# Attention stage of a fused attention, MLP and expert kernel: where ScalarE's exponential and VectorE's side work stand in the scheduler's order

## The chip, the cores and the metric

The kernel runs on one core of a Trainium2 chip. The metric is the time of one execution in microseconds of device time. Three executions of the kernel before took 960.75, 962.94 and 966.66 us; their median is 962.94 us.

## The reference

Causal attention over 4 batches, 8 heads, 576 positions and a head size of 64 is mixed with a memory read-out and goes through a dense MLP and then through one of eight expert MLPs. The change lies in the attention.

```python
scores = scale * np.matmul(q, k.transpose(0, 1, 3, 2))
scores = np.where(causal, -1000000000.0, scores)
a = np.exp(scores - scores.max(-1, keepdims=True))
a /= a.sum(-1, keepdims=True) + 1e-09
local = np.matmul(a, v)
q_p = phi(q)                       # phi(x) = where(x > 0, x, exp(x) - 1) + 1
mem_out = einsum(q_p, M_prev) / (einsum(q_p, z_prev)[..., None] + 1e-06)
attn = g * mem_out + (1 - g) * local          # g = sigmoid(beta), per head
x = attn.transpose(0, 2, 1, 3).reshape(B * S, H * D)
x = np.maximum(x @ w_in, 0.0) ** 2 @ w_out
...
```

After this each row of x is routed to its best of 8 experts (normalized dot products, softmax weight), and the expert's two matmuls with a ReLU between them give the output.

## The kernel before, in words

**Stages.** The attention comes first (about 0 to 384 us of the trace); the first half of the dense MLP is laid between its steps. The rest of the MLP, the routing and the experts follow. Each float32 matmul is made of three matmuls of rounded parts (names ending in `h` and `l` are the high and the low part of a tile).

**Pairs and units.** The heads are taken in 16 pairs of two, numbered 0 to 15 here. A pair has nine units, in the order of ORDER: unit 0 has the last 64 rows of both heads (`h` is None, tile `A8`), then come (head, block of 128 rows): (0,3), (1,3), (0,0), (1,0), (0,2), (1,2), (0,1), (1,1). A unit is a chain over four engines:
- TensorE makes the scores into `ps` (`scores`, L446, matmuls L476);
- VectorE copies them to `A` under the mask and takes the row minimum of their negatives into `nm` in the same instruction (L480, "the minimum" below; a second short instruction reads `nm` out);
- ScalarE makes the exponential of `A` in place with its row sums `sm` (L486);
- VectorE makes the reciprocal of the sums (L494 and L495, or L489 and L490), for both heads of a block at once;
- GpSimd scales `A` by it (L437);
- five units later TensorE transposes `A` into a PSUM tile `pt` (`turn`, L442). It is one of two buffers of the pool `psT` (tag T, L195), which also hold the transposes of the features of the next pair (`tk`, `tq`, `t2`, `tp`, `t3`);
- ScalarE copies `pt` to SBUF (`ATa`, `ATb`, `AT`, L619), and eight units after its scores the unit is multiplied with the values (`values`, L538, L570).

**The features of the next pair** (`prep`, L301) run beside the units: `e` is the exponential of q (ScalarE, L349); `phi` (L352 to L354) finishes it on VectorE; GpSimd multiplies by z into `u` (L358); `norm` (L387) sums `u` on VectorE into `nr` (L388), adds and inverts it (L390, L392); GpSimd multiplies `e` by `nr` (L396); TensorE transposes `e` into `tp` (L403). The transposes `t2` of the last rows are copied by ScalarE to `hk` and `qbh` (L368, L371), and VectorE makes their low parts `kl` and `qbl` (L374, L377).

**The MLP's part.** `step` lays one half step of the MLP into most units: the first layer (12 matmuls L742; then ScalarE's ReLU `r` L746, VectorE's square L750, ScalarE's rounding `gh` L751 and VectorE's remainder `gl` L752), or the second layer (6 matmuls L776 to L778, which read `gh` and `gl`). In pairs 9, 11, 13 and 15 the next chunk of x is split: `xh` on ScalarE (L719), `xl` on VectorE (L720).

**What sets the order.** The loop over t (t = 9 * pair + unit, from L607) writes instructions unit by unit. `later` puts functions aside for a later t and an engine's list: "act0" and "dve0" are run ahead of the unit's minimum and exponential, "act", "dve" and "pool" behind them (`due`, L594). What is written is not always what each engine gets: TensorE's order is always the written one; ScalarE's, VectorE's, GpSimd's and SyncE's are the written ones only up to t = 8 (STRICT = 9, L608), VectorE's and GpSimd's up to t = 71 (FREE = 72, L611). From there on a scheduler places each instruction as early as its own estimates say that its inputs are there. t = 72 is the first unit of pair 8. `pinned` (L79) is a context in which each new instruction of an engine is placed behind the last one written so far for that engine.

In the loop (L628 to L643) the unit whose scores were written last is `here`, the one ahead of it is `before`. The first `next(here)` writes the minimum, the second the exponential; `next(before)` writes the sums' reciprocals and the scaling.

Of the kernel before, what the change touches and what calls it, by code (L numbers as in the profile page):

```python
# [19 lines left out]
ENG = mybir.EngineType  # L20
# [38 lines left out]
FREE = 72  # L59
STRICT, BUSY = 9, {-5: 14, 0: 12, 2: 6, 4: 4, 5: 4, 6: 4, 7: 4}  # L60
# [31 lines left out]
@contextmanager  # L92
def pinned(tc, *engines):

    with ExitStack() as ctx:
        for e in engines:
            last = next((i for i in reversed(tc.nc.cur_bb.bb.instructions) if i.engine == e), None)
            if last is not None:
                ctx.enter_context(tc.issue_after(last))
        yield  # L100
# [87 lines left out]
def attention(tc, sh, q, k, v, M, z, beta, w_in, w_out, mlp, step):  # L188

    nc = tc.nc  # L190
    with ExitStack() as ctx:
# [44 lines left out]
        def load(p):  # L236
            b, hp = divmod(p, NPP)
            qn_, kn_ = naturals.get(p, (qn, kn))
            fetch(p, (k, kn_), (q, qn_))
            zb = st.tile([128, 128], F32, name="zb", tag="zb")  # L240
            nc.sync.dma_start(zb, z[b:b + 1, 2 * hp:2 * hp + 2].rearrange("o h d -> o (h d)").to_broadcast([128, 128]))
            nat[p] = (vns[p % 3], zb, Mts[p % 3], qn_, kn_)

        def load_values(p):
            b, hp = divmod(p, NPP)
            fetch(p, (v, vns[p % 3]))
            for h in range(2):
                hs = slice(h * 64, h * 64 + 64)
                nc.sync.dma_start(Mts[p % 3][hs, hs], M[b, 2 * hp + h])
# [23 lines left out]
        def mix():  # L273

            nc.scalar.activation(g_all, g_all, AF.Exp, scale=-1.0)
            nc.vector.tensor_scalar_add(gi, g_all, 1.0)
            nc.vector.reciprocal(g_all, gi)
            nc.vector.tensor_scalar(g1, g_all, -1.0, 1.0, ALU.mult, ALU.add)
            for h in range(2):
                hs = slice(h * 64, h * 64 + 64)  # L280
                nc.vector.tensor_copy(g2[hs], g1.rearrange("p (a h) -> p h a", h=2)[hs, h])
# [309 lines left out]
        conv = conversions2(nc, st, sh, 0, nc.gpsimd, w_in, w_out)  # L591
        units = [(p, h, r) for p in range(NPAIR) for h, r in ORDER]

        def due(eng):  # L594
            for f in queue.pop((t, eng), ()):
                f()

        def busy(n):

            w = psX.tile([128, 512], F32, name="w", tag="X")  # L600
            for _ in range(n):
                nc.tensor.transpose(w[:, :128], ident, ident)

        here, before, gens, t = None, None, [prep(0)], -EARLY
        while t < len(units) + LP + 5 or queue:
            now[0] = t
            p, i = divmod(t, 9)  # L607
            if t == STRICT:  # L608
                strict.close()
                strict.enter_context(tc.manual_schedule(engines={ENG.DVE, ENG.Pool}))  # L610
            if t == FREE:  # L611
                strict.close()
            if t in BUSY:
                busy(BUSY[t])
            start = START[min(p, 2)]
            if 0 <= p < NPAIR - 1 and i == start:
                gens.append(prep(p + 1))
            for d, x in evacs:
                nc.scalar.copy(d, x)  # L619
            evacs.clear()  # L620
            due("act0")
            if here is not None:
                next(here)
            due("dve0")
            if here is not None:
                next(here)
            if before is not None:
                next(before)  # L628
            before, here = here, None
            if t == MIX:  # L630
                mix()
            if t == AHEAD:
                next(conv)
            due("act")
            due("dve")
            due("pool")
            if t > CONV[0] and t % 9 != CONV[1] and next(conv, conv) is not conv:
                sh.converted += 1
            n = t - LP
            if n % 9 == 0 and (n - 1) // 9 in JOINED:  # L640
                values(*units[n - 1])
            if 0 <= n < len(units) and (n % 9 < 8 or n // 9 not in JOINED):
                values(*units[n])  # L643
            if 0 <= p < NPAIR - 2 and i == 8:
                load_values(p + 2)
            if t % 9 != REST:
                step(t)
            for g in list(gens):
                if next(g, gens) is gens:
                    gens.remove(g)  # L650
            if 0 <= p < NPAIR - 2 and i == start + 5:
                load(p + 2)
            if 0 <= t - LT < len(units):
                turn(*units[t - LT])
            if 0 <= t < len(units):
                here = scores(*units[t])
                next(here)
            for f in behind_scores:
                f()
            behind_scores.clear()  # L660
            t += 1
# [752 lines left out]
def tile_kernel(ctx, tc, q, k, v, M, z, beta, w_in, w_out, emb, tau, w1, w2, out):  # L1414
# [16 lines left out]
    with ExitStack() as mctx:  # L1431
# [17 lines left out]
        with tc.manual_schedule(engines={ENG.PE}):  # L1449
            attention(tc, sh, q, k, v, M, z, beta, w_in, w_out, mlp, step)  # L1450
# [63 lines left out]
```

## Time and profile before

| what | value |
|---|---|
| median of three executions | 962.94 us (960.75 to 966.66) |
| profiled execution: its own time, its span | 954.52 us, 952.4 us |
| TensorE busy | 898.4 us, 94% of the span |
| TensorE's weight loads | 787.3 us, 83% |
| VectorE, ScalarE, GpSimd busy | 594.3 us, 525.0 us, 293.2 us |
| mean granted TensorE clock | 0.989 of full speed |

The span reaches from the first to the last instruction; 2.1 us of the profiled execution lie around it. The profiled execution is 8.4 us below the median of the three others. Starts in the trace are counted from the span's start. A wait is given with the engine and tile that ended it; where an instruction waits for several things, the one that came last is named.

### The profile page before, as it was taken

The numbers are of one execution on the slowest core, as the hardware profiler recorded it, in microseconds if no ns is written. First come the engines' busy times: TensorE is split into PE (matmuls) and PEld (weight loads), VectorE is DVE, ScalarE is ACT, GpSimd is POOL, SyncE is SP. The second block draws the span as 40 slices with busy tenths as digits, with TensorE's granted clock in tenths as the row PEclk, the third lists the DMA queues.
The fourth block names the chain that finished last, engine by engine and source line by source line (L and its number), as shares of the span: only waits on it lengthen the run. The fifth ranks groups of instructions, "written<-read, shape, count | busy, mean of one in ns | idle before, by whom it ended". The sixth has DMA issues, their size and how long they took to land.

```text
span 952.4 us, 19266 instructions
## 1 busy us (share of the span) xinstructions
PE 898.4 (94%) x6319; PEld 787.3 (83%) x6319; DVE 594.3 (62%) x1737; ACT 525.0 (55%) x1363; POOL 293.2 (31%) x356
## 2 busy tenths in 40 slices
PE   7878899999999999999999999999999999999993
PEld 6766677888888888898798888888899999999983
DVE  4689878655555654587527778889772535353551
ACT  4787778776666667576655555665421424242440
POOL 4466657333334432000311111433311311111111
PEclk9999899999999999999999999999999999999997
DMA  6677666444344420244310112521060635352521
GB/s 175 152 176 186 154 158 155 118 101 114 86 110 92 116 56 23 70 153 156 112 62 35 61 45 82 174 67 47 33 222 20 199 113 161 102 174 91 181 78 35
DMA packets 107081, 105.81 MB, mean 111 GB/s; under 512 B 66095, under 2 KB 76335, under 8 KB 106944
## 3 DMA queue, kind: packets, MB, share of 16 engines
q1 hardware_dynamic: 100528, 89.13, 34.0%
q0 software_dynamic: 4544, 13.67, 4.4%
q10 hardware_dynamic: 1872, 1.34, 0.5%
q8 instruction: 66, 1.08, 0.5%
q14 instruction: 71, 0.58, 0.2%
HBM read 70.80 MB, written 14.70 MB: 90 GB/s over the span
## 4 chain that ended last, share of the span: by engine, by line
PE 66%; DVE 14%; issue 7%; DMA 6%; ACT 4%; POOL 2%; SPq 1%; POOLq 0%; ACTq 0%; DVEq 0%
PE ps L742 16%; PE psh L1309 11%; PE y L776 5%; PE y L778 5%; PE y L777 5%; PE ps L476 4%; PE psy L1325 3%; PE psy L1327 3%; PE psy L1326 3%; PE xo L570 3%; PE pt L442 2%; DMA raw<-in_moe_w_out_dram 2%; DVE A L480 2%; DMA raw<-in_moe_w_in_dram 2%; DVE x L879 1%
## 5 line engine op out<-in xcount | busy, mean ns | idle before, releaser
L437 POOL TENSOR_SCALAR A<-A,sm,g 128x512 f32<-128x512 f32 (+4 forms) x108 | 80.5, 754 | 134.7 <-DVE sm L495 61.0
L486 ACT ACTIVATE A<-A,nm 128x576 f32<-128x576 f32 (+2 forms) x144 | 84.7, 588 | 63.2 <-DVE nm L480 27.2
L742 PE MATMUL ps<-xh,Wh 128*128 128x256 f32 x416 | 118.3, 284 | 0.4 <-ACT r L746 0.4
L742 PE MATMUL ps<-xh,Wl 128*128 128x256 f32 x416 | 117.5, 282 | 0.0
L742 PE MATMUL ps<-xl,Wh 128*128 128x256 f32 x416 | 117.5, 282 | 0.0
L776 PE MATMUL y<-Wh,gh 128*128 128x512 f32 x288 | 115.6, 401 | 0.0
L778 PE MATMUL y<-Wh,gl 128*128 128x512 f32 x288 | 113.7, 395 | 1.3 <-DVE es L1037 1.1
L777 PE MATMUL y<-Wl,gh 128*128 128x512 f32 x288 | 113.4, 394 | 0.0
L1311 ACT ACTIVATE hh<-psh 128x512 fp32r<-128x512 f32 x44 | 26.4, 599 | 144.1 <-PE psh L1309 81.3
L752 DVE TENSOR_TENSOR gl<-r,gh 128x256 fp32r<-128x256 f32 x144 | 66.5, 463 | 59.6 <-ACT gh L751 57.7
L1309 PE MATMUL psh<-xTh,Wh 128*128 128x256 f32 x352 | 99.2, 282 | 0.7 <-PEq L1317 0.7
L1309 PE MATMUL psh<-xTh,Wl 128*128 128x256 f32 x352 | 98.8, 281 | 0.2 <-DVE Wl L114 0.2
L1309 PE MATMUL psh<-xTl,Wh 128*128 128x256 f32 x352 | 98.7, 280 | 0.0
L746 ACT ACTIVATE r<-ps 128x256 f32<-128x256 f32 x144 | 54.9, 382 | 77.4 <-PE ps L742 67.6
L480 DVE CUSTOM_DVE_ANT_0 A<-ps,mask 128x256 f32<-128x256 f32 (+4 forms) x160 | 75.1, 477 | 30.9 <-PE ps L476 30.3
L1312 DVE SCALAR_TENSOR_TENSOR hl<-psh,hh 128x512 fp32r<-128x512 f32 x44 | 30.4, 690 | 92.7 <-ACTq L1299 38.1
L742 PEld LDWEIGHTS ps<-xh,Wh 128*128 128x128 f32 x416 | 78.8, 190 | 3.6 <-ACT r L746 0.8
L742 PEld LDWEIGHTS ps<-xl,Wh 128*128 128x128 f32 x416 | 79.0, 190 | 2.6
L742 PEld LDWEIGHTS ps<-xh,Wl 128*128 128x128 f32 x416 | 79.2, 190 | 0.0
L751 ACT CAST gh<-r 128x256 fp32r<-128x256 f32 x144 | 58.3, 405 | 34.1 <-PE y L777 32.4
L1309 PEld LDWEIGHTS psh<-xTh,Wh 128*128 128x128 f32 x352 | 66.2, 188 | 2.2 <-ACTq L1299 1.1
L778 PEld LDWEIGHTS y<-Wh,gl 128*128 128x128 f32 x288 | 54.1, 188 | 16.1 <-DVE gl L752 1.5
(348 smaller groups left out, 2422.1 us busy)
## 6 DMA issues: line engine op xcount, KB each, us to landing
x<-in_moe_w_dram SPq DMA_DIRECT2D x48, 512.0 KB, 9.3
ks<-hk SPq DMA_DIRECT2D x60, 128.0 KB, 2.4
raw<-in_moe_w_in_dram SPq DMA_DIRECT2D x15, 512.0 KB, 3.6
raw<-in_moe_w_out_dram SPq DMA_DIRECT2D x15, 512.0 KB, 4.1
x2d<-x SPq DMA_DIRECT2D x18, 256.0 KB, 2.4
vn<-in_v_dram SPq DMA_DIRECT2D x32, 128.0 KB, 3.0
x2p<-x SPq DMA_DIRECT2D x16, 256.0 KB, 3.5
part<-x2p SPq DMA_DIRECT2D x16, 256.0 KB, 3.4
```

What stands on the lines that cost most here:

```text
L437: nc.gpsimd.tensor_scalar(A, A, a, b, ALU.mult, ALU.mult)
L476: nc.tensor.matmul(ps[:, :wide], x, y[:, a:a + wide], start=j == 0, stop=j == len(terms) - 1)
L480: nc.vector.tensor_tensor_reduce(A[:, a:a + w], tiles[j][:, :w], mask[:, end - w:end], -1.0, 3e38, ALU.add, ALU.min, nm[:, j:j + 1])
L486: nc.scalar.activation(A[:, :n], A[:, :n], AF.Exp, bias=nm[:, 0:1], scale=-1.0, accum_out=sm[:, i:i + 1])
L742: nc.tensor.matmul(ps[:, :CH], a, b, start=n == 0, stop=n == len(ops) - 1)
L746: self.later(1, "act", lambda: nc.scalar.activation(r, ps[:, :CH], AF.Relu))
L751: self.later(3, "act", lambda: nc.scalar.copy(gh, r))
L752: self.later(3, "dve", lambda: nc.vector.tensor_tensor(gl, r, gh.bitcast(F32), ALU.subtract))
L776: nc.tensor.matmul(y, gh[:, sl], wh, start=first, stop=False)
L777: nc.tensor.matmul(y, gh[:, sl], wl, start=False, stop=False)
L778: nc.tensor.matmul(y, gl[:, sl], wh, start=False, stop=last)
L1309: nc.tensor.matmul(ps[:, a], w[kc][:, sl], x[:, kc], start=kc + j == 0, stop=kc + j == 5)
```

## The change

`then(eng)` gives a `pinned` context for one engine, or nothing: for ScalarE from t = 9 on, for VectorE from t = 72 on. Three places of the loop are put into it: the exponential goes behind the ScalarE instructions written ahead of it in its unit; the sums' reciprocals of the unit before (`next(before)`) and the list "dve" (features, sums, the MLP's squares, remainders and splits) go behind the VectorE instructions written ahead of them, the last of which is the unit's minimum.

```diff
+        def then(eng):
+
+            if t < STRICT or (eng == ENG.DVE and t < FREE):
+                return nullcontext()
+            return pinned(tc, eng)
...
             due("dve0")
-            if here is not None:
-                next(here)
-            if before is not None:
-                next(before)
+            with then(ENG.Activation):
+                if here is not None:
+                    next(here)
+            with then(ENG.DVE):
+                if before is not None:
+                    next(before)
             before, here = here, None
...
             due("act")
-            due("dve")
+            with then(ENG.DVE):
+                due("dve")
             due("pool")
```

What this makes of the engines' orders is seen in pair 9; pairs 10 to 14 read much alike. In the lists below numbers tell buffers apart, and lines of the changed kernel from L594 on are 6 to 9 higher (L625, L729, L759, L760 and L761 are L619, L720, L750, L751 and L752 of before).

**VectorE, units 5 and 6 of pair 9.** `A_3217` is unit (0,2), `A_3258` is (1,2); `e_3175`, `u_3176` and `nr_3177` are the features of pair 10, `t2_3241` their last rows. Before:

```order
L353 TENSOR_SCALAR e_3175<-e_3175 128x640
L494 SCALAR_TENSOR_TENSOR sm_3138<-sm_3138,mask_146 128x2
L354 SCALAR_TENSOR_TENSOR e_3175<-qn_122,e_3175 128x640
L495 RECIPROCAL sm_3138<-sm_3138 128x2
L388 TENSOR_REDUCE nr_3177<-u_3176 128x10
L480 ISA A_3217,nm_3218<-ps_3220,mask_146 128x384
L480 ISA nm_3218 128x1
L390 SCALAR_TENSOR_TENSOR nr_3177<-nr_3177,gi_189 128x10
L392 RECIPROCAL nr_3177<-nr_3177 128x10
L374 TENSOR_TENSOR kl_3042<-t2_3241,hk_3043 128x64
L377 SCALAR_TENSOR_TENSOR qbl_135<-t2_3241,qbh_134 64x64
L480 ISA A_3258,nm_3259<-ps_3260,mask_146 128x384
```

The same stretch in the changed kernel:

```order
L761 TENSOR_TENSOR gl_3084<-r_3082,gh_3083 128x256
L480 ISA A_3217,nm_3218<-ps_3220,mask_146 128x384
L480 ISA nm_3218 128x1
L494 SCALAR_TENSOR_TENSOR sm_3138<-sm_3138,mask_146 128x2
L495 RECIPROCAL sm_3138<-sm_3138 128x2
L759 TENSOR_TENSOR r_3162<-r_3162 128x256
L353 TENSOR_SCALAR e_3175<-e_3175 128x640
L354 SCALAR_TENSOR_TENSOR e_3175<-qn_122,e_3175 128x640
L374 TENSOR_TENSOR kl_3042<-t2_3241,hk_3043 128x64
L480 ISA A_3258,nm_3259<-ps_3260,mask_146 128x384
L480 ISA nm_3259 128x1
L377 SCALAR_TENSOR_TENSOR qbl_135<-t2_3241,qbh_134 64x64 x2
```

The minimum of (0,2) now stands ahead of the sums, the square and the features; `nr` (L388, L390, L392) has left the stretch and stands three minima further down, behind that of unit (1,1).

**ScalarE, the same place.** `ATa_3253` is the copy of the transposed unit (0,3), `hk` and `qbh` take the last rows of the next pair, `gh_3163` is the MLP's. Before, and then the changed kernel:

```order
L619 COPY AT4_3216<-pt4_3214 128x128
L486 ACTIVATE A_3217,sm_3219<-A_3217,nm_3218 128x384
L368 CAST hk_3043<-t2_3241 128x64
L371 ACTIVATE qbh_134<-t2_3241 64x64 x2
L751 CAST gh_3163<-r_3162 128x256
L619 COPY ATa_3253<-pt_3252 128x4x128
```

```order
L625 COPY AT4_3216<-pt4_3214 128x128
L486 ACTIVATE A_3217,sm_3219<-A_3217,nm_3218 128x384
L760 CAST gh_3163<-r_3162 128x256
L368 CAST hk_3043<-t2_3241 128x64
L371 ACTIVATE qbh_134<-t2_3241 64x64 x2
L625 COPY ATa_3253<-pt_3252 128x4x128
```

Only the rounding `gh` has moved, from behind the copies of the last rows to ahead of them. The exponential stands where it stood.

**VectorE, units 1 and 2 of pair 9**, where the next chunk of x is split into `xl0` to `xl3`. `A_3055` is unit (0,3) and `A_3102` is (1,3). Before, and then the changed kernel:

```order
L480 ISA A_3055,nm_3056<-ps_3058,mask_146 128x512
L480 ISA nm_3056 128x1
L720 TENSOR_TENSOR xl0_3086<-x1_2_92,xh0_3085 128x256
L720 TENSOR_TENSOR xl1_3088<-x1_2_92,xh1_3087 128x256
L720 TENSOR_TENSOR xl2_3090<-x1_2_92,xh2_3089 128x256
L330 SCALAR_TENSOR_TENSOR lq_3045<-tq_3093,hq_3044 128x512
L480 ISA A_3102,nm_3103<-ps_3104,mask_146 128x512
L480 ISA nm_3103 128x1
L720 TENSOR_TENSOR xl3_3092<-x1_2_92,xh3_3091 128x256
L752 TENSOR_TENSOR gl_3084<-r_3082,gh_3083 128x256
```

```order
L480 ISA A_3055,nm_3056<-ps_3058,mask_146 128x512
L480 ISA nm_3056 128x1
L489 SCALAR_TENSOR_TENSOR sm_3012<-sm_3012,mask_146 128x1
L490 RECIPROCAL sm_3012<-sm_3012 128x1
L330 SCALAR_TENSOR_TENSOR lq_3045<-tq_3093,hq_3044 128x512
L480 ISA A_3102,nm_3103<-ps_3104,mask_146 128x512
L480 ISA nm_3103 128x1
L761 TENSOR_TENSOR gl_3006<-r_3004,gh_3005 128x256
L729 TENSOR_TENSOR xl0_3086<-x1_2_92,xh0_3085 128x256
L729 TENSOR_TENSOR xl1_3088<-x1_2_92,xh1_3087 128x256
L729 TENSOR_TENSOR xl2_3090<-x1_2_92,xh2_3089 128x256
L729 TENSOR_TENSOR xl3_3092<-x1_2_92,xh3_3091 128x256
```

The first three parts of the split now stand behind the minimum of (1,3) and a remainder of the MLP, one unit later than before.

Elsewhere: TensorE's order is the same instruction for instruction. ScalarE's is the same up to pair 8, so through the whole of t = 9 to 71, where it alone is pinned. On GpSimd the product `e` by `nr` (L396) moves from ahead of the scalings of (0,2) and (1,2) to behind them. On SyncE the next load of q (L256, L258), which overwrites what L354 reads, moves behind the load of k's last rows.

## Rows read from the trace of the kernel before

**Rows 1.** Busy us (count) by stretch: PE, PEld, DVE, ACT, POOL; PEclk, DMA.

```profile
192.00:216.00 24.00, 24.00 (x192) 20.92 (x191) 13.41 (x49) 18.40 (x55) 9.39 (x12) 1.00 0.45 102
216.00:240.00 24.00, 22.55 (x178) 19.29 (x177) 13.27 (x48) 15.40 (x45) 7.92 (x10) 1.00 0.46 112
```

**Rows 2.** Waits of TensorE, 192 to 384 us: total us, times, longest.

```profile
PE pt L442 <- ACT ATa L619: 8.8, 6, 1.5
```

**Rows 3.** Timeline: start, us, engine, line, tiles; first scores of three pairs.

```profile
182.31 0.39 PE L476 MATMUL ps<-hk,qbh 128*128 128x320 f32 x1
...
205.74 0.39 PE L476 MATMUL ps<-hk,qbh 128*128 128x320 f32 x1
...
356.05 0.39 PE L476 MATMUL ps<-hk,qbh 128*128 128x320 f32 x1
```

**Rows 4.** Timeline, all engines, unit (0,2) of pair 9 and behind.

```profile
219.59 0.34 PE L476 MATMUL ps<-kl,qz 128*128 128x384 f32 x1
...
219.88 1.57 POOL L358 TENSOR_TENSOR u<-e,zb 128x640 f32<-128x640 f32 x1
...
221.48 0.82 DVE L388 TENSOR_REDUCE nr<-u 128x10 f32<-128x640 f32 x1 [2.62 <-POOL u L358]
...
222.22 0.55 DVE L480 CUSTOM_DVE_ANT_0 A<-ps,mask 128x384 f32<-128x384 f32 x1
...
222.87 0.62 ACT L486 ACTIVATE A<-A,nm 128x384 f32<-128x384 f32 x1 [2.61 <-DVE nr L390]
...
224.47 0.59 ACT L619 COPY ATa<-pt 128x512 f32<-128x512 f32 x1
...
225.20 0.63 PE L442 MATMUL pt<-ident,A 128*128 128x128 f32 x4 [1.45 <-ACT ATa L619]
```

**Rows 5.** Timeline, all engines, unit (0,2) of pair 8 and behind.

```profile
196.16 0.34 PE L476 MATMUL ps<-kl,qz 128*128 128x384 f32 x1
...
196.53 0.56 DVE L480 CUSTOM_DVE_ANT_0 A<-ps,mask 128x384 f32<-128x384 f32 x1 [0.53 <-PE ps L476]
...
197.13 0.62 ACT L486 ACTIVATE A<-A,nm 128x384 f32<-128x384 f32 x1 [0.31 <-DVE nm L480]
...
197.75 0.41 ACT L751 CAST gh<-r 128x256 fp32r<-128x256 f32 x1
...
198.72 0.59 ACT L619 COPY ATa<-pt 128x512 f32<-128x512 f32 x1
...
200.16 0.60 PE L442 MATMUL pt<-ident,A 128*128 128x128 f32 x4
```

**Rows 6.** Timeline, the product by nr, the last minimum and tp.

```profile
223.28 1.26 POOL L396 TENSOR_TENSOR e<-e,nr 128x640 f32<-128x640 f32 x1 [1.83 <-DVE nr L392]
...
229.76 0.42 DVE L480 CUSTOM_DVE_ANT_0 A<-ps,mask 128x256 f32<-128x256 f32 x1
...
238.37 0.60 PE L403 MATMUL tp<-ident,e 128*128 128x128 f32 x4
```

**Rows 7.** Waits of TensorE's weight loads, whole span.

```profile
PEld tp L403 <- POOL e L396: 5.9, 2, 3.4
```

**Rows 8.** Timeline, VectorE and TensorE, units 2 and 3 of pair 9.

```profile
212.77 0.68 DVE L480 CUSTOM_DVE_ANT_0 A<-ps,mask 128x512 f32<-128x512 f32 x1
...
213.38 0.42 DVE L720 TENSOR_TENSOR xl<-x,xh 128x256 fp32r<-128x256 f32 x1
...
214.09 0.28 PE L742 MATMUL ps<-xl,Wh 128*128 128x256 f32 x1
```

**Rows 9.** Timeline, the MLP's square in two units of pair 9.

```profile
215.14 1.53 POOL L437 TENSOR_SCALAR A<-A,sm,g 128x512 f32<-128x512 f32 x2 [5.29 <-ACT pT L404]
...
216.02 0.92 DVE L750 TENSOR_TENSOR r<-r 128x256 f32<-128x256 f32 x1 [1.07 <-ACT r L746]
...
225.71 0.16 DVE L494 SCALAR_TENSOR_TENSOR sm<-sm,mask 128x2 f32<-128x2 f32 x1
...
225.99 0.42 DVE L750 TENSOR_TENSOR r<-r 128x256 f32<-128x256 f32 x1
```

## Prediction

> **What bounds the kernel now.** I read the stretches first, then TensorE's waits, then the length of the pairs, then the timeline around the wait. From 192 us TensorE is the bound: it is busy for 24.00 of 24 us at full clock in pair 8 and the start of pair 9, and for 22.55 in the next stretch [rows 1]. What it misses there is one wait per pair, six times 1.45 us, at the transposes `pt` behind ScalarE's copy `ATa` [rows 2, 4]. The length of the pairs puts a better price on it. Pair 8, which has no such wait, takes 205.74 - 182.31 = 23.43 us; pairs 9 to 14 take (356.05 - 205.74) / 6 = 25.05 us [rows 3]. TensorE's share of a pair is the same, so a wait costs 25.05 - 23.43 = 1.62 us, more than the 1.45 of the wait row, whose ends of matmuls are modelled. Six of them are 9.7 us, and that is all that TensorE has to gain in the part of the program that moves.
>
> Where does the wait come from? In pair 9 the scores of unit (0,2) end at 219.59 + 0.34 = 219.93, but their minimum starts at 222.22, since `nr` (L388) stands ahead of it and has itself waited 2.62 us for GpSimd's `u`, which started at 219.88 [rows 4]. The exponential waits 2.61 us for the minimum; behind it on ScalarE stand the copies of the last rows, `gh`, and then `ATa`, which ends at 224.47 + 0.59 = 225.06; TensorE goes on at 225.20, because the transposes of (1,3) need the PSUM buffer that `ATa` empties. In pair 8 the order already had the minimum ahead of `nr`: it starts 0.03 us after the scores (196.50), `ATa` ends at 199.31, and the transposes at 200.16 have not waited [rows 5].
>
> **The change part by part.** *ScalarE, t = 9 to 71:* no instruction moves, so nothing is paid or gained there.
>
> *The minimum ahead of the features, pairs 9 to 14.* I lay pair 9 out anew. The minimum starts at 219.96 and, as in pair 8, the exponential 0.60 later, at 220.56. From the exponential to the end of `ATa` pair 8 takes 199.31 - 197.13 = 2.18 us [rows 5], with the order that pair 9 now gets (`gh`, the last rows, `ATa`): 222.74. One thing differs: `gh` reads VectorE's square, which stands behind the sums. The minimum occupies VectorE for 0.56; from the sums' start to the square's end are 225.99 - 225.71 + 0.42 = 0.70 [rows 9]; the square ends at 221.22 and ScalarE would begin `gh` at 220.56 + 0.62 = 221.18: 0.04 late. So `ATa` ends at 222.8. TensorE comes to the transposes of (1,3) 4.00 us after the start of the last scores of (0,2), if nothing holds it (200.16 - 196.16 [rows 5]): at 223.59. There are 0.8 us to spare, and the wait goes: 6 x 1.62 = 9.7 us.
>
> *What is late next: the split.* In pairs 9, 11 and 13 `xl0` now comes behind the minimum of (1,3) and one `gl`. This minimum leaves VectorE at 213.38, where `xl3` starts today; `gl` and `xl0` are two instructions of 0.42 us, so `xl0` is there at 213.38 + 0.84 = 214.22, and TensorE asks for it at 214.09 [rows 8]. That is 0.13 us, three times, 0.4 us; the parts behind it follow faster than TensorE needs them. Pair 15 has no `lq` ahead of the minimum, and keeps time.
>
> *GpSimd's product (L396)*, now behind the scalings of (0,2) and (1,2), with `nr` behind the minimum of (1,1): that minimum starts at 229.76; with 0.42 for itself, 0.42 for a square, 0.82 for L388 [rows 4], twice 0.2 for L390 and L392 (an estimate from the spacing of the sums' two instructions, 0.28 up to the next but one [rows 9]) and 1.26 for the product it is done by 233.1. TensorE wants it for `tp` at 238.37 [rows 6]. 5 us hide it: 0. If that cover were gone, a wait for it has cost up to 3.4 us in the early pairs [rows 7].
>
> *The sums and scalings* come up to one unit later (25.05 / 9 = 2.8 us); their tiles are transposed five units after the scores, so 0. *`qbl`* stands behind one more minimum, 0.55 us, and is next wanted a unit later: 0. *The load of q* on SyncE waits for L354, which is 3 to 4 us later than before, and its transposes come at unit 2 of the next pair, some five units away: 0.
>
> *What could cost more.* Not seen in the trace is the new neighbourhood: square and features now run just as GpSimd begins the scalings of units (0,0) and (1,0). The nearest row is a square beside a scaling: 0.92 us where another takes 0.42 [rows 9]. So an instruction placed there costs between 0 and 0.50 us more; I take 0, as the 0.8 us above would cover one such loss, and keep 0.50 for the range. [...]
>
> Sum: -9.7 + 0.4 = -9.3 us. The profiled execution goes from 954.52 (span 952.4 and 2.1 around it) to 945.2 us. Its own time lies 8.4 us below the median of the runs shown; I take the same 9.3 us from that median: 962.9 - 9.3 = 953.6 us. Everything after the attention waits for TensorE or comes in its train, so the gain should last to the end.
>
> **The rivals.**
> *A. The wait comes back in part.* `gh`, and behind it `ATa`, now hang on VectorE's square. If the square, the sums ahead of it or the copies are hit by more than the 0.8 us to spare, TensorE waits again. For it: the row of 0.92, and that the square had stood behind the copies before. Against: it takes two losses of 0.50 in one unit. Price: half of each wait stays, 6 x 0.8 = 4.9, and the split is hit too, 3 x (0.13 + 0.50) = 1.9; 9.7 - 6.8 = 2.9 us gained, 960.0 us.
> *B. Slower: `tp` becomes the wait.* If the product came over 5.3 us later than I have it (GpSimd is in order, and it now waits for sums that wait for the exponential of (1,2)), `tp` would stand still once per pair, pairs 8 to 14. At 3.4 us [rows 7] that is 7 x 3.4 = 23.8 us for 9.7 saved: 977 us. The point where it turns to a loss is a wait of 1.4 us per pair. Against: 5 us of cover.
> *C. Nothing comes of it.* The pinning for ScalarE moves nothing by itself, and what VectorE's part frees could be eaten where buffers come round, another wait of 1.6 us per pair in place of the old: 962.9 us. Against: pair 8 runs at 23.43 us with nearly the new order.
>
> **How the numbers follow.** A measurement of this kernel can tell about 1% (9.6 us) from no change. Forecast 0.70: its 9.3 us lie just under that line, with 9.7 as the most there is and runs that scatter by 0.3%, so I put 0.35 on each side of it. A 0.16, within 1%. C 0.09, 0.08 of it within 1% and 0.01 slower. B 0.05, slower. Faster by over 1%: 0.35; within: 0.35 + 0.16 + 0.08 = 0.59; slower: 0.06. The range runs from 950.5 (all of 9.7, and the 2.2 us by which the lowest run lies under the median, and a little) to 960.5 (A); it leaves out B and C, 0.14, and little below.
>
> **What would show it.** Right: TensorE's wait at `pt` behind `ATa` is gone from pairs 9 to 14; the pairs take 23.4 to 23.6 us; the minimum of (0,2) starts within 0.1 us of its scores; small waits of TensorE for `xl` in pairs 9, 11 and 13. Wrong: pairs of 24 us or more, TensorE waiting for `ATa` behind `gh` (A), for `e` at `tp` (B), or for anything else once per pair (C), or a stretch after 384 us that grows by what the attention loses.

## The result, and the profile after

| | before | changed | ratio, 95% interval |
|---|---|---|---|
| first measurement, median | 961.85 us (960.06 to 966.66, four executions) | 953.12 us (950.55 to 954.08, four) | 0.9897, 0.9855 to 0.9939 |
| second measurement, later | 963.23 us (958.76 to 971.03, eleven) | 952.33 us (946.75 to 956.16, six) | 0.9885, 0.9844 to 0.9926 |
| the profiled execution, its span | 954.52 us, 952.4 us | 954.08 us, 952.4 us | |

The ratio is an estimate on record with its interval, and not the quotient of the two medians beside it, which is 0.9909 in the first row and 0.9887 in the second. The changed kernel is about 1% faster, 953.12 us where 953.6 was forecast. Yet the two profiled executions have the same span, so I cut both into three parts. Pairs are counted here from the start of VectorE's first minimum of `A8`, as its rows are complete in every trace (some of TensorE's are missing).

| part of the span | before | changed |
|---|---|---|
| start to pair 8 (order the same, but for VectorE's last 6 us) | 183.36 us | 192.30 us |
| pair 8 to pair 15 | 173.57 us | 164.53 us |
| pair 15 to the end | 595.47 us | 595.57 us |

The rows that it is cut at, before and then changed:

```profile
183.36 0.47 DVE L480 CUSTOM_DVE_ANT_0 A<-ps,mask 128x320 f32<-128x320 f32 x1
...
356.93 0.48 DVE L480 CUSTOM_DVE_ANT_0 A<-ps,mask 128x320 f32<-128x320 f32 x1
```

```profile
192.30 0.49 DVE L480 CUSTOM_DVE_ANT_0 A<-ps,mask 128x320 f32<-128x320 f32 x1 [0.47 <-PE ps L476]
...
356.83 0.49 DVE L480 CUSTOM_DVE_ANT_0 A<-ps,mask 128x320 f32<-128x320 f32 x1
```

The middle part, where the change moves instructions, is 9.04 us shorter. The first part is 8.94 us longer, with the same instructions, and in the same order up to its last 6 us, where `nr` already stands behind two more minima and TensorE waits in neither kernel. The section on the hardware comes back to it. The windows of the changed kernel that answer to [rows 1] (same columns):

```profile
192.00:216.00 24.00, 24.00 (x190) 20.91 (x189) 12.64 (x46) 17.21 (x53) 9.64 (x12) 1.00 0.45 101
216.00:240.00 24.00, 24.00 (x188) 20.69 (x187) 14.58 (x54) 18.32 (x54) 9.61 (x12) 1.00 0.53 119
```

TensorE is now busy for the whole 24 us in both. The wait of [rows 2] has gone, and the table of TensorE's waits from 192 to 384 us has no row left. The starts of pairs 8, 9, 10 and 15, as in [rows 3]:

```profile
191.58 0.39 PE L476 MATMUL ps<-hk,qbh 128*128 128x320 f32 x1
...
215.01 0.39 PE L476 MATMUL ps<-hk,qbh 128*128 128x320 f32 x1
...
238.64 0.39 PE L476 MATMUL ps<-hk,qbh 128*128 128x320 f32 x1
...
356.11 0.39 PE L476 MATMUL ps<-hk,qbh 128*128 128x320 f32 x1
```

Pair 8 takes 23.43 us as before, pair 9 takes 23.63. Pairs 9 to 14 take 356.11 - 215.01 = 141.10 us, where they took 150.31: 9.21 us less. The timeline of the changed kernel at unit (0,2) of pair 9, which answers to [rows 4]:

```profile
229.06 0.34 PE L476 MATMUL ps<-kl,qz 128*128 128x384 f32 x1
...
229.53 0.56 DVE L480 CUSTOM_DVE_ANT_0 A<-ps,mask 128x384 f32<-128x384 f32 x1 [3.15 <-PE ps L476]
...
230.13 0.62 ACT L486 ACTIVATE A<-A,nm 128x384 f32<-128x384 f32 x1 [0.41 <-DVE nm L480]
...
230.29 0.41 DVE L759 TENSOR_TENSOR r<-r 128x256 f32<-128x256 f32 x1
...
230.78 0.41 ACT L760 CAST gh<-r 128x256 fp32r<-128x256 f32 x1
...
231.67 0.59 ACT L625 COPY ATa<-pt 128x512 f32<-128x512 f32 x1
...
232.29 1.56 POOL L358 TENSOR_TENSOR u<-e,zb 128x640 f32<-128x640 f32 x1
...
233.01 1.12 DVE L761 TENSOR_TENSOR gl<-r,gh 128x256 fp32r<-128x256 f32 x1
233.06 0.60 PE L442 MATMUL pt<-ident,A 128*128 128x128 f32 x4
```

The minimum starts 0.13 us behind its scores (2.29 before), the exponential 0.60 later, `ATa` ends at 232.26, and TensorE comes to the transposes at 233.06 without waiting. The remainder `gl` takes 1.12 us beside GpSimd's `u`, but nothing waits for it here.

### The profile page after: what moved, and what is told of

Read it like the earlier page. It is cut to its first block, busy times and chain, and to the rows that moved or that the text cites. A ratio compares the mean times of both kernels' runs of the same rounds, so it can differ in the third digit from the quotient of the medians.

```text
span 952.4 us, 19267 instructions
## 1 busy us (share of the span) xinstructions
PE 904.4 (95%) x6319; PEld 791.8 (83%) x6319; DVE 599.2 (63%) x1737; ACT 527.8 (55%) x1363; POOL 293.3 (31%) x356
## 3 DMA queue, kind: packets, MB, share of 16 engines
q10 hardware_dynamic: 1872, 1.34, 0.5%
## 4 chain that ended last, share of the span: by engine, by line
PE 72%; issue 5%; DVE 5%; DMA 3%; ACT 1%; POOL 1%; SPq 0%; POOLq 0%; DVEq 0%; ACTq 0%
PE ps L751 18%; PE psh L1318 11%; PE y L785 6%; PE y L787 6%; PE y L786 6%; PE ps L476 4%; PE xo L570 3%; PE psy L1334 3%; PE psy L1336 3%; PE psy L1335 3%; PE pt L442 3%; DMA raw<-in_moe_w_in_dram 1%; DMA raw<-in_moe_w_out_dram 1%; PE xo L549 1%; DVE wt L146 1%
## 5 line engine op out<-in xcount | busy, mean ns | idle before, releaser
L480 DVE CUSTOM_DVE_ANT_0 A<-ps,mask 128x256 f32<-128x256 f32 (+4 forms) x160 | 75.5, 480 | 96.6 <-PE ps L476 95.2
L751 PE MATMUL ps<-xh,Wh 128*128 128x256 f32 x416 | 119.0, 286 | 0.1
L751 PE MATMUL ps<-xl,Wh 128*128 128x256 f32 x416 | 118.3, 284 | 0.0
L751 PE MATMUL ps<-xh,Wl 128*128 128x256 f32 x416 | 118.0, 284 | 0.0
L761 DVE TENSOR_TENSOR gl<-r,gh 128x256 fp32r<-128x256 f32 x144 | 71.0, 494 | 33.4 <-ACT gh L760 32.9
L751 PEld LDWEIGHTS ps<-xh,Wh 128*128 128x128 f32 x416 | 79.8, 192 | 3.4 <-ACT r L755 0.5
L751 PEld LDWEIGHTS ps<-xl,Wh 128*128 128x128 f32 x416 | 79.8, 192 | 3.1 <-DVE xl L729 0.2
L751 PEld LDWEIGHTS ps<-xh,Wl 128*128 128x128 f32 x416 | 79.8, 192 | 0.0
L760 ACT CAST gh<-r 128x256 fp32r<-128x256 f32 x144 | 58.3, 405 | 33.7 <-PE y L786 31.3
L1334 PE MATMUL psy<-Wh,hh 128*128 128x512 f32 x168 | 67.1, 399 | 0.1
```

The costliest lines, as they stand in the source:

```text
L480: nc.vector.tensor_tensor_reduce(A[:, a:a + w], tiles[j][:, :w], mask[:, end - w:end], -1.0, 3e38, ALU.add, ALU.min, nm[:, j:j + 1])
L751: nc.tensor.matmul(ps[:, :CH], a, b, start=n == 0, stop=n == len(ops) - 1)
L760: self.later(3, "act", lambda: nc.scalar.copy(gh, r))
L761: self.later(3, "dve", lambda: nc.vector.tensor_tensor(gl, r, gh.bitcast(F32), ALU.subtract))
L1334: nc.tensor.matmul(y[h], xh, wh, start=g + a == 0, stop=False)
```

## The experiments

Theory 1: the whole gain is that the minimum of (0,2) no longer stands behind `nr` in pairs 9 to 14. The rivals give a part to ScalarE's half, to the sums, to the features, or to chance in the early part. Ratios are to the kernel before on the same chip.

**ScalarE's half alone.**

```diff
-            if t < STRICT or (eng == ENG.DVE and t < FREE):
+            if t < STRICT or eng == ENG.DVE:
```

> The change with ScalarE's half alone (the exponential pinned, VectorE free). The order of every engine comes out as in the kernel before. Theory 1 (the whole gain is VectorE's minimum of unit (0,2) standing ahead of nr in pairs 9 to 14): nothing changes, ratio 0.996 to 1.004 to before, pairs 9 to 14 take 25.05 us each with the 1.45 us wait at pt behind ATa. Rival (ScalarE's half has a part in it): ratio below 0.995 and pairs shorter than 25. As the program is that of before, the start of pair 8 shows besides how far the early part scatters by itself: with the granted clock at its full level throughout I expect about 182 us, with low stretches up to 192.

Measured: 1.0011 (0.9977 to 1.0044); pair 8 to 15 in 173.53 us (before: 173.57), the six waits for `ATa` still there. Every engine's order is that of before: ScalarE's half moves nothing, and this was in effect the kernel before once more. The start of pair 8 came at 188.48 us, 5.1 later than in the profile before.

**The sums alone** (`due("dve")` free, ScalarE free).

```diff
             with then(ENG.DVE):
                 if before is not None:
                     next(before)
...
-            with then(ENG.DVE):
-                due("dve")
+            due("dve")
```

> Of VectorE's half only the sums' reciprocals are pinned behind the minimum; features, squares, remainders and splits stay free, and nr (L388) stays ahead of the minimum of (0,2) in pairs 9 to 14. Theory 1: the wait stays, pairs 9 to 14 take 25.0 to 25.3 us, ratio to before 0.997 to 1.003. Rival (what matters is that the minimum is not held by the sums, or the new order as a whole): pairs of 23.4 to 24.2 us, ratio 0.99 to 0.995.

Measured: 0.9973 (0.9942 to 1.0004), pairs 9 to 14 of 24.03 us. My expectation was wrong: the wait did not stay, it shrank to 0.41 us, and the pairs fall into the rival's range. (By the ratio alone this kernel cannot be told from the one before.) TensorE's waits from 195 to 384 us:

```profile
PE pt L442 <- ACT ATa L625: 2.4, 6, 0.5
```

and the timeline of pair 9 in this kernel:

```profile
229.73 0.83 DVE L354 SCALAR_TENSOR_TENSOR e<-qn,e 128x640 f32<-128x640 f32 x1
...
230.64 1.56 POOL L358 TENSOR_TENSOR u<-e,zb 128x640 f32<-128x640 f32 x1 [2.18 <-DVE e L354]
...
231.39 0.34 PE L476 MATMUL ps<-kl,qz 128*128 128x384 f32 x1
...
232.23 0.82 DVE L388 TENSOR_REDUCE nr<-u 128x10 f32<-128x640 f32 x1 [1.68 <-POOL u L358]
232.97 0.55 DVE L480 CUSTOM_DVE_ANT_0 A<-ps,mask 128x384 f32<-128x384 f32 x1
...
235.23 0.59 ACT L625 COPY ATa<-pt 128x512 f32<-128x512 f32 x1
...
235.96 0.63 PE L442 MATMUL pt<-ident,A 128*128 128x128 f32 x4 [0.41 <-ACT ATa L625]
```

`nr` still stands ahead of the minimum, but with the sums later GpSimd makes `u` ahead of the scalings, right behind L354, and `nr` waits 1.68 us for it instead of 2.62. The minimum is 1.24 us late instead of 2.29. So pinning the sums helps only by making `nr` less late.

**The list "dve" alone** (`next(before)` and ScalarE free; the reverse of the last one: `next(before)` stands outside the context, `due("dve")` in it).

> The other part of VectorE's half: the list (features, nr, squares, remainders, splits) is pinned behind the minimum, the sums' reciprocals are free. nr stands behind the minimum of (1,1), as in the changed kernel. Theory 1 (nr ahead of the minimum of (0,2) is the whole wait): pairs 9 to 14 take 23.43 us, the odd ones 23.63 for the split; no wait at pt. Rival (the sums too must be behind the minimum): pairs of 23.9 us or more.

Measured in one execution, the profiled one: pairs 10 to 14 of 23.43, 23.63, 23.39, 23.62 and 23.39 us, no wait at `pt`. In pair 9 TensorE waited 0.6 us for `xl`, so that one took 24.30, 0.67 more than expected. The sums need not be pinned.

**`nr` alone**, all else as before.

```diff
             def norm():
-                nc.vector.tensor_reduce(nr, u.rearrange("p c (h d) -> p (c h) d", h=2), AX.X, ALU.add)
+                with pinned(tc, ENG.DVE) if now[0] >= FREE else nullcontext():
+                    nc.vector.tensor_reduce(nr, u.rearrange("p c (h d) -> p (c h) d", h=2), AX.X, ALU.add)
```

> The kernel before with one edit: from pair 8 on nr (L388) is pinned behind the last VectorE instruction written; sums, squares, features and the split of x stay free. Theory 1: this alone gives the whole gain, and without the small wait for xl: pairs 9 to 14 all take 23.43 us, ratio to before 0.989 (6 x 1.62 = 9.7 us less), 0.6 us under the changed kernel. Rival (squares and features must leave too, since they hold the minimum or ATa by themselves): part of the wait stays, pairs of 23.9 us or more, ratio 0.993 or more.

Measured: 0.9915 (0.9888 to 0.9942), where the quotient of the medians, 951.83 / 964.14, is 0.987; no wait of TensorE from 195 to 384 us; pairs 9 to 14 in 140.64 us, 23.44 on average. The starts of pairs 9 and 15 (L481 is L480 of before):

```profile
211.12 0.49 DVE L481 CUSTOM_DVE_ANT_0 A<-ps,mask 128x320 f32<-128x320 f32 x1
...
351.76 0.49 DVE L481 CUSTOM_DVE_ANT_0 A<-ps,mask 128x320 f32<-128x320 f32 x1
```

One pinned instruction per pair gives the whole gain, without the price of the split. Squares, features and sums need not be pinned for it.

**The split free**, all else as in the changed kernel.

```diff
-            with then(ENG.DVE):
-                due("dve")
+            for f in queue.pop((t, "dve"), ()):
+                with nullcontext() if f in mlp.free else then(ENG.DVE):
+                    f()
```

(`mlp.free` lists the functions that write `xl`.)

> The changed kernel, but the split of x (xl) is not pinned and stands one unit earlier again, ahead of the minimum of (1,3). Theory: the 0.2 us by which pairs 9, 11 and 13 are longer than pairs 8, 10, 12 and 14 is TensorE's wait for xl; all seven pairs take 23.4 us, 0.6 us less in all, ratio to before 0.988 to 0.990. Rival (xl ahead of lq and the minimum of (1,3) delays these, or the 0.2 us is the extra work of a split): odd pairs stay at 23.6 us or get longer.

Measured: 0.9904 (0.987 to 0.9937); pairs 9 to 14 of 23.43, 23.44, 23.43, 23.39, 23.40 and 23.39 us, 140.48 in all. The 0.2 us of the odd pairs was the wait for `xl`.

**The minimum made late**, in the changed kernel. The second edit holds ScalarE's copy `ATa` in its written place, which in the timeline is right behind the exponential.

```diff
                 end = 768 if h is not None else 256 if j else 576
+                if (h, r) == (0, 2) and 9 <= p <= 14:
+                    for _ in range(6):
+                        nc.vector.tensor_reduce(nm[:, j:j + 1], tiles[j][:, :256], AX.X, ALU.min)
...
             for d, x in evacs:
-                nc.scalar.copy(d, x)
+                with pinned(tc, ENG.Activation) if i == 7 and 9 <= p <= 14 else nullcontext():
+                    nc.scalar.copy(d, x)
```

> The changed kernel with six extra VectorE reductions of the score tile (128x256 from PSUM, about 0.4 us each, results overwritten) ahead of the minimum of (0,2) in pairs 9 to 14: the minimum is late on purpose, with no nr and no GpSimd in it. ATa now stands right behind the exponential, gh behind the next one. So far: minimum 2.29 us behind its scores gave 1.62 us per pair (before), 1.24 us gave 0.60 (sums alone): one for one, some 0.65 us free; with gh (0.41) gone from ahead of ATa about 1.05 free. Theory 1 (it is the minimum's lateness that TensorE waits for, whatever makes it late): 2.5 to 2.9 us late, pairs of 24.9 to 25.3 us with a wait at pt behind ATa. Rival (the wait was GpSimd's or nr's own and the minimum's lateness is harmless): pairs stay at 23.4 to 23.6.

Measured in one execution, the profiled one: pairs of 24.73 to 24.99 us (149.16 / 6 = 24.86). The timeline of pair 9 (five of the six reductions are in one row):

```profile
226.95 0.34 PE L476 MATMUL ps<-kl,qz 128*128 128x384 f32 x1
227.32 2.26 DVE L482 TENSOR_REDUCE nm<-ps 128x1 f32<-128x256 f32 x5 [3.05 <-PE ps L476]
...
230.21 0.56 DVE L483 CUSTOM_DVE_ANT_0 A<-ps,mask 128x384 f32<-128x384 f32 x1
...
231.54 0.59 ACT L629 COPY ATa<-pt 128x512 f32<-128x512 f32 x1
...
232.27 0.41 PE L442 MATMUL pt<-ident,A 128*128 128x128 f32 x2 [1.16 <-ACT ATa L629]
```

The wait is back with no `nr` in it. Four kernels now give one account. TensorE starts the transposes 0.14 us behind the end of `ATa`, and comes to them 233.06 - 229.40 = 3.66 us behind the end of the scores when nothing holds it:

| pair 9 | minimum behind its scores | minimum's start to `ATa`'s end | sum + 0.14 - 3.66 | longer per pair, measured |
|---|---|---|---|---|
| before | 2.29 us | 2.84 | 1.61 | 25.05 - 23.43 = 1.62 |
| sums alone | 1.24 us | 2.85 | 0.57 | 24.03 - 23.43 = 0.60 |
| six more | 2.92 us | 1.92 | 1.32 | 24.86 - 23.52 = 1.34 |
| changed | 0.13 us | 2.73 | -0.66 | 0 |

(23.52 is the changed kernel's mean, 141.10 / 6.) The account holds to 0.03 us in the three kernels with a wait, and gives none in the fourth, from which the 3.66 us are taken. I had expected 24.9 to 25.3 us for the late minimum, a little too much: I had not counted that the copies of the last rows, too, have left the place ahead of `ATa`.

**Fillers against the early loss of clock** (with `nr` pinned): identity transposes into tiles that the next real ones overwrite.

```diff
             tp = new_T(p, "tp")
+            for _ in range(14 if p in (0, 2, 3) else 0):
+                nc.tensor.transpose(tp[:, :128], ident, ident)
...
+                for _ in range(8 if (h, r) == (0, 2) and 1 < p < 4 or (h, r) == (1, 2) and 2 < p < 6 else 0):
+                    nc.tensor.transpose(p4[:, 0], ident, ident)
                 for j in range(r + 1):
                     flip(p4[:, r - j], A[:, j * 128:j * 128 + 128], d)
```

> nr alone pinned, and in the early pairs 82 filler transposes of the identity on TensorE, written into PSUM tiles that the next real transposes overwrite, at places where TensorE has stood still 1.4 to 3.2 us in the profiles (14 ahead of tp for pairs 0, 2 and 3; 8 ahead of pt of unit (0,2) in pairs 2 and 3 and of unit (1,2) in pairs 3 to 5). In the six profiles so far the start of pair 8 goes with the mean granted clock of 0 to 192 us: 183 to 195 us at 0.97 to 0.91, about 178 us plus (1 - clock) x 192. Theory (the clock falls behind these waits and the fillers hold it): mean clock 0.96 or more, pair 8 from 180 to 185 us, ratio to before 0.980 to 0.986. Rival 1 (TensorE's order is filled where nothing waits: 82 x 0.11 to 0.15 = 9 to 12 us more work, most of it not hidden): ratio 0.993 or more. Rival 2 (the clock falls at the other waits all the same): as with nr alone, 0.990 to 0.992.

Measured: 0.9951 (0.9929 to 0.9974), pair 8 at 198.72 us, mean clock 0.93: rival 1 came true, the fillers cost time. Nor did the clock gain: over the whole execution its mean is 0.980 in the twelve with fillers and 0.980 in the nine with `nr` alone. At 84.94 us TensorE waited 2.3 us ahead of a filler, since the tile itself was not free, and the clock was at 0.50 by then (columns as in [rows 1]):

```profile
84.00:86.00 2.00, 1.06 (x5) 1.09 (x6) 1.97 (x6) 1.47 (x4) 1.61 (x3) 0.50 0.24 49
```

So these fillers stood behind the wait and not in it, and so did those of pair 2, behind a wait of 2.9 us. Whether work inside such a wait would hold the clock, or fillers other than transposes would, is not tested.

**`nr` behind the minimum in the early pairs too** (with `nr` pinned from pair 8 on). In the early pairs the written order decides. In the changed kernel's profile VectorE has this between the scores of pair 7's `A8` (ended at 166.84) and their minimum:

```profile
166.53 0.81 DVE L388 TENSOR_REDUCE nr<-u 128x10 f32<-128x640 f32 x1
167.37 1.02 DVE L390 SCALAR_TENSOR_TENSOR nr<-nr,gi 128x10 f32<-128x10 f32 x1
168.43 0.22 DVE L392 RECIPROCAL nr<-nr 128x10 f32<-128x10 f32 x1
168.56 0.63 DVE L146 SCALAR_TENSOR_TENSOR wt<-raw,wt 128x512 int32<-128x512 int32 x1
169.11 0.48 DVE L480 CUSTOM_DVE_ANT_0 A<-ps,mask 128x320 f32<-128x320 f32 x1
```

```diff
-            later(1, "dve", norm)
-            later(1, "pool", lambda: ...
+            late = 2 if 27 <= now[0] < FREE - 2 else 1
+            later(late, "dve", norm)
+            later(late, "pool", lambda: ...
```

> nr alone pinned from pair 8 on, and besides, in the early pairs whose order is the written one (t = 27 to 69), nr and GpSimd's product by it are written one unit later, behind the minimum of A8 instead of ahead of it. In the profiles nr (0.81 + 1.02 + 0.22) and a step of the weight conversion (0.63) stand there between the scores of A8 of pair 7 and their minimum, and TensorE waits 2.05 us for it (about 164 to 170 us in every profile), with a fall of the granted clock to its half behind it in most. Theory (the same mechanism as in pairs 9 to 14): this wait goes or falls under 1 us, in pairs 5 and 6 some tenths go as well; 2 to 5 us less than with nr alone, ratio to before 0.986 to 0.990. Rival (VectorE is the bound of the early pairs, so a wait only changes its place: nr now stands ahead of the minimum of (0,3)): the start of pair 8 stays at 178 us plus lost clock, ratio 0.990 to 0.993.

Measured: 0.9871 (0.9827 to 0.9915). The wait of 2.05 us is gone, but pair 8 starts at 190.92 us with a mean clock of 0.94, inside the spread of the others. On that chip the median was 951.73 us against the changed kernel's 952.33, which the scatter hides. The ratio lies in the theory's range, but `nr` alone was not run on that chip. Whether it gains anything stays open.

**The changed kernel once more.**

> The changed kernel once more, for a narrower interval and a further profile. Theory 1: pair 8 to the start of pair 15 takes 164.5 us as in the first profile (173.5 before), so 9.0 us less than before; ratio to before 0.9906, and what the profiled execution differs by from that of the first profile lies in the start of pair 8 alone, with the mean granted clock of 0 to 192 us (about 178 us plus (1 - clock) x 192). Rival (the first measurement of 0.9897 owed something to chance in the early part): ratio outside 0.9875 to 0.9935.

Measured: 0.9885, inside the bounds; pair 8 to 15 in 164.52 us, 0.01 from the first profile.

## Why the prediction was right, point by point

- *TensorE's wait, -9.7 us.* Right in place and size. In the four kernels with this part and without the price of the split, pairs 9 to 14 take 140.48 to 140.64 us by the minima, where before took 150.47: 9.8 to 10.0 us. The step that `nr` is the cause is shown by `nr` alone; that the minimum's lateness is what TensorE pays for, by the table of four kernels. The minimum starts 0.13 us behind its scores, where within 0.1 was the sign given.
- *`ATa` with 0.8 us to spare.* It ends 0.80 us ahead of TensorE's transposes, as laid out; less the 0.14 that TensorE starts behind it, 0.66 is free.
- *The split, +0.4 us.* The right mechanism, under-sized: the odd pairs are 0.2 us longer, 3 x 0.2 = 0.6, and with the split free this is gone. The table of TensorE's waits has no row for it, as it hides in the matmuls: the first one on `xl` starts 0.21 us behind the one on `xh` and takes 0.38 us instead of 0.28. The rows of pair 9, VectorE and TensorE:

```profile
222.65 0.42 DVE L761 TENSOR_TENSOR gl<-r,gh 128x256 fp32r<-128x256 f32 x1
...
222.98 1.43 DVE L729 TENSOR_TENSOR xl<-x,xh 128x256 fp32r<-128x256 f32 x4
...
223.25 0.28 PE L751 MATMUL ps<-xh,Wh 128*128 128x256 f32 x1
...
223.46 0.38 PE L751 MATMUL ps<-xl,Wh 128*128 128x256 f32 x1
```

- *ScalarE's half, sums, `qbl`, load of q: 0.* Right; the first is shown by a kernel of its own, the others only by the length of the pairs.
- *GpSimd's product, 5 us of cover.* Right: in the changed profile it starts at 215.41 us, takes 1.26, and `tp` is transposed at 222.58, 5.9 us later. Rival B had no place.
- *New neighbourhood, 0 to 0.50 us an instruction, taken as 0.* Beside the scalings this held: the square, on which rival A rested, took 0.41 us, and it was GpSimd that lost (its two scalings beside square and features took 1.78 us, where before they took 0.89). The prediction did not look beside `u`, where `gl` lost 1.12 - 0.42 = 0.70 us, more than its bound.
- *Sum -9.3 us.* Pairs 9 to 14 lost 9.21 us. The medians differ by 8.7 and 10.9 us, on both sides of it. That the median came within 0.5 us of the forecast is partly luck, as the four executions lie between 950.55 and 954.08 us. The forecast for the profiled execution failed: 945.2 us against 954.08. It took over the early part of one profile, which came 8.94 us later in the other; the prediction had not seen that the early part scatters by up to 11 us between profiles.

## What to carry to other kernels

Look at what stands, on its own engine, ahead of the instruction that the bound engine's chain goes through: here one reduction on VectorE that waited for a third engine, once per pair (2.62 us in pair 9, where the minimum behind it started 2.29 us late), was the whole difference, and pinning that one instruction did as much as pinning dozens. Price a wait by the length of the stage with and without it, and lay the chain out against the time at which the bound engine comes for it; that gave three kernels' waits to 0.03 us. And when two profiles have the same span, cut them by stage before believing that nothing changed.

## What the runs showed of the hardware

**The first 190 us scatter, for the most part by the granted clock, with the same work.** The stretch up to pair 8, for before and then for the changed kernel (columns as in [rows 1]):

```profile
0.00:183.36 183.36, 156.40 (x1213) 129.80 (x1214) 139.65 (x425) 133.91 (x376) 107.82 (x136) 0.97 0.67 161
```

```profile
0.00:192.30 192.30, 162.39 (x1211) 133.65 (x1212) 141.01 (x423) 134.34 (x377) 106.17 (x136) 0.93 0.63 154
```

Of the 8.94 us by which they differ, 5.99 are busy time of TensorE, with the same matmuls at the lower mean clock, and 2.95 are idle time. In the nine profiles whose early part is that of before, pair 8 starts at 183.36 us with 0.97; 187.61 and 188.48 with 0.95; 190.19 with 0.94; 192.02, 192.30 and 192.93 with 0.93; 193.41 and 194.82 with 0.91. These are mean clocks of 0 to 192 us; (1 - clock) x 192 accounts for each of them to within 2 us, counted from 178. The 178 is fitted, and part of the low clock falls on time in which TensorE stands still, so this describes the nine and does not show what made each of them late. From pair 15 on, all eleven profiles took 594.0 to 596.2 us. Behind TensorE's wait in pair 7 the granted clock fell to 0.50 in seven of these nine profiles; before and with the sums alone it stood at 1.00 up to the next scores. The wait and the next scores of that kind, before and then changed:

```profile
161.83 0.50 PE L476 MATMUL ps<-ks,qs 128*128 128x512 f32 x1 [2.05 <-DVE nm L480]
...
164.52 0.48 PE L476 MATMUL ps<-ks,qs 128*128 128x512 f32 x1
```

```profile
169.66 0.80 PE L476 MATMUL ps<-ks,qs 128*128 128x512 f32 x1 [2.05 <-DVE nm L480]
...
173.78 0.48 PE L476 MATMUL ps<-ks,qs 128*128 128x512 f32 x1
```

Two microseconds behind it, before and then changed (columns as in [rows 1]):

```profile
162.00:164.00 2.00, 2.00 (x16) 1.91 (x17) 1.93 (x9) 1.48 (x5) 1.89 (x4) 1.00 0.93 204
```

```profile
170.00:172.00 2.00, 2.00 (x9) 1.81 (x9) 1.64 (x6) 1.31 (x4) 1.89 (x5) 0.50 0.96 209
```

The same wait, then 2.69 us to the next scores in the one and 4.12 in the other, where the clock stood at 0.50. With the sums alone it was 2.69 again, in the six others 3.78 to 4.24. No run here shows what decides whether the clock falls. In the seven profiles that have a fall, it comes between 0.2 us ahead of the start of these scores and 1.5 us behind it, read from the granted clock in windows of half a microsecond. This wait thus cost its own length and, in seven profiles of nine, 1.1 to 1.6 us more.

**A VectorE instruction beside GpSimd lost more than I had allowed for, 1.35 us against 0.50.** The conversion step L141 next to `u`, and the same step on its own, in the changed kernel's early part:

```profile
91.89 1.55 POOL L358 TENSOR_TENSOR u<-e,zb 128x640 f32<-128x640 f32 x1 [0.62 <-DMA qz<-hq]
91.96 1.76 DVE L141 TENSOR_SCALAR wt<-wt 128x512 f32<-128x512 f32 x1
...
117.24 0.41 DVE L141 TENSOR_SCALAR wt<-wt 128x512 f32<-128x512 f32 x1
```

It took 1.76 us where it takes 0.41 on its own: it lost 1.35 us, nearly the whole of `u`, which had started 0.07 us ahead of it and took 1.55. No run shows by what means. My bound of 0.50, from one row beside a scaling, is too small beside `u`; in pairs 9 to 14 it did no harm, as nothing that TensorE waits for was hit.
